# A Mamba-2 scan with an ELU feed-forward behind it: high word of y on ScalarE, scan steps, weight words, loads and output copies moved within their queues

## The chip, the cores and the metric

The kernel runs on one core of a Trainium2 chip. The metric is device time in microseconds, the median of several executions; lower is better. The names are those of the profile: PE is TensorE's matmul row and PEld its weight load, DVE is VectorE, ACT is ScalarE, POOL is GpSimd, SP is the engine whose queue issues nearly all DMAs. Each engine works through its own instructions strictly in program order, so the place of an instruction in its engine's queue matters as much as its length.

## The reference

Two blocks follow each other. The first is a chunked state-space scan over 4 batches, 8 heads, 768 tokens, head size 32, state size 16. The second is a feed-forward layer over all 3072 tokens, with 256 model columns and 2048 hidden ones:

```python
M = CB * L                                   # scores times decays, per chunk and head
y_intra = np.einsum('bhij,bhjd->bhid', M, xc)
y_inter = np.einsum('bhin,bhnd->bhid', Cc, state) * decay_to_i[:, :, :, None]
state = decay_full[:, :, None, None] * state + np.sum(Bx, axis=2)
...
h = x @ w_in                                 # x is y of the scan, one row a token
g = np.where(h > 0.0, h, alpha * (np.exp(np.minimum(h, 0.0)) - 1.0))
return (g @ w_out).astype(np.float32)
```

## The kernel before

**Tiling.** The tokens are cut into 12 blocks of 256. Blocks 0 and 1 fill the pipeline with plain fp32 products; from block 2 on, blocks go in pairs. A *stage* n (4, 6, 8, 10 in the main loop, L1357 on) does three things at once, interleaved by hand: the first feed-forward product and the ELU of pair n, the second product of pair n-2, and the scan of pair m = n+2. After stage 10 a tail does the second product of the last pair.

**Words.** An fp32 product is put together from three passes over rounded words. For y: `y1` is the high word (scaled copy, rounded to fp32r), `y0` the low one (L804), `y_both` a combination (L814); for the weights and for g there are the same three. The passes give `high` and `both`, and the result is `high * (WORD - 1) + WORD * both`.

**Groups.** Inside a stage, k counts 16 *groups*, each 128 hidden columns by 512 tokens, made by `l1_words(n, k, m)` (L819): six matmuls into two PSUM banks, `ps_w` (the `both` sum) and `ps_h` (the `high` one). Then a loop over DVE and ACT closes each group: ACT copies `ps_w` to `e` (L838), DVE finishes the group before it (L861, `end_words`), DVE joins `ps_h` and `e` (the *join*, L844), ACT takes a Relu and an Exp of the joined bank (L854, L855, `begin_end`), and the next group's L861 waits for that Exp. A bank is free again when its last reader is through: `ps_w` after L838, `ps_h` after L861.

**Jobs.** The words of g for the second product are made in three steps spread over two groups: ACT's high word (L916, `first_of_jobs`), DVE's low word (L917, `second_of_jobs`), POOL's combination (L893, `third_of_jobs`). Job q is begun in group q-3 and PE reads it three groups later with twelve short matmuls (L975, two steps of `second`, `l2s(2)`). When a block's sum is complete, `put_out` copies it out: ACT (L981), DVE (L984), then the DMA (L986); its two halves are queued by `put_first` and `put_second`.

**Scan of the next pair.** `stage_scan` places small steps on ACT, DVE, POOL and SP in groups 0 to 10 (POOL's decay masks, L561 and L544, stand in groups 0 to 3). Then come, in this order: `scores` (64 small matmuls, L577, after group 9), `weigh_two` for four quarters (DVE, L586; each frees one bank of scores), `sums` (L607), `states` (DVE L622 and L624, POOL L629), `across` (L654), `inside` in two halves t (L672), and the copies of the result to `yT` (ACT L689 for t = 0, DVE L687 for t = 1). After that, in groups 14 and 15, the words of y are made for the next stage, whose first matmul passes need them.

**PSUM.** Pool `ps_a` has seven banks, `ps_o` has one, used in turn by a sum of `second`, the last quarter of the scores, half of the sums and the last quarter of `across`.

**SP's queue.** `load_words(i)` brings back the words of `w_in` piece i (512 KB, L759, and 256 KB, L760), used by groups 2i and 2i+1. Pieces 0 and 1 of the next stage are loaded in groups 14 and 15, behind a 64-byte DMA named `held` (L1385), which reads a few elements of `yT` and so keeps SP's queue until they are written; piece 2 is loaded in group 0, behind that group's output DMAs. In stage 4 the words of `w_out` pieces 3 to 7 are still being made (`words_of_out`: ACT L902, DVE L903; `low_of_out`: POOL L893).

## Time and profile before

| | |
|---|---|
| median of 3 runs | 347.2 us (346.45 to 347.7) |
| profiled execution, whole | 348.19 us |
| its span (first to last instruction) | 346.5 us |
| granted TensorE clock, mean | 0.999 |
| first stage of the main loop, groups 0 to 15 | 113.9 to 168.0 us |
| stage 6 | 168.0 to 221.5 us |
| stage 8 | 221.5 to 273.9 us |
| stage 10 | 273.9 to 320.2 us |
| tail | 320.2 to 346.5 us |

A stage starts where the trace has the first `ps_h` matmul of its group 0. Busy time by stretch of 20 us (us of work in the stretch):

| stretch | PE | DVE | ACT | POOL |
|---|---|---|---|---|
| 120 to 140 | 20.00 | 15.87 | 17.74 | 16.13 |
| 140 to 160 | 19.03 | 19.14 | 13.97 | 16.60 |
| 160 to 180 | 19.14 | 16.50 | 15.63 | 14.89 |
| 180 to 200 | 19.91 | 19.41 | 16.11 | 16.59 |
| 200 to 220 | 19.63 | 15.20 | 12.95 | 12.75 |
| 220 to 240 | 19.82 | 18.72 | 16.91 | 15.88 |
| 240 to 260 | 20.00 | 17.96 | 15.57 | 13.62 |
| 260 to 280 | 18.80 | 15.96 | 13.91 | 8.78 |
| 280 to 300 | 20.00 | 16.23 | 17.45 | 11.41 |
| 300 to 320 | 20.00 | 18.43 | 16.74 | 13.18 |

How to read the profile's lines: a group's line gives line number, engine, operation, `written<-read` tiles, shapes and count, then busy time and the mean of one in ns, then the idle time before them and what ended it. A line of the timeline begins with start and length in us; a bracket at its end is the idle time of that engine just before, with the work that ended it. Matmuls are pipelined: their rows overlap, and PE counts as busy from the start of one to the modelled end of the next, so a short wait can hide in a busy row.

### The profile page before, as it was taken

To read this page: it belongs to the slowest core of one execution; us is meant where nothing else is said; L and a number is where in the kernel's file an instruction comes from. 1 tells how busy PE (TensorE), PEld (TensorE's weight loads), DVE (VectorE), ACT (ScalarE), POOL (GpSimd) and SP (SyncE) were. 2 spreads that over 40 slices of the span, in tenths; PEclk is the share of its full clock that TensorE was granted. 3 is DMA by queue.
4 is the path that set the end of the run, shared out by engine and by line. 5 is a ranking of instruction groups with operands and counts; after the bars stand their busy time and mean duration, and the time that the engine had idled before them with its cause. 6 is when DMAs were issued, how large, how long until landed. Compare 5 with 4: busy or idle time off the path is not lost.

```text
span 346.5 us, 9640 instructions
## 1 busy us (share of the span) xinstructions
PE 336.4 (97%) x3742; PEld 290.8 (84%) x3742; DVE 288.8 (83%) x511; ACT 258.1 (75%) x533; POOL 214.4 (62%) x242
## 2 busy tenths in 40 slices
PE   8899999999999999899999999999999899999996
PEld 6568888888888888788788888898888799999995
DVE  2898998889997778997999986999986877997951
ACT  4798989599756888866698865797866689897601
POOL 4653554648989396978498858498855245675100
PEclk9999999999999999999999999999999999999999
DMA  8998988472487486631569692569550664160101
GB/s 143 243 218 181 304 174 248 89 134 98 163 159 284 150 241 224 237 101 27 182 180 208 172 305 52 184 196 217 138 182 3 184 208 151 52 199 0 33 0 62
DMA packets 82956, 54.79 MB, mean 158 GB/s; under 512 B 59038, under 2 KB 68574, under 8 KB 82910
## 3 DMA queue, kind: packets, MB, share of 16 engines
q1 hardware_dynamic: 80734, 53.98, 55.8%
q8 instruction: 29, 0.48, 0.6%
q10 hardware_dynamic: 2176, 0.20, 0.5%
q14 instruction: 17, 0.14, 0.1%
HBM read 44.53 MB, written 9.63 MB: 156 GB/s over the span
## 4 chain that ended last, share of the span: by engine, by line
PE 75%; DVE 7%; ACT 5%; SPq 4%; DMA 4%; issue 2%; POOL 1%; DVEq 0%; POOLq 0%; ACTq 0%
PE ps_o L975 18%; PE ps_h L830 14%; PE ps_h L711 11%; PE ps_o L879 11%; PE ps_w L830 8%; PE ps_both L975 6%; DMA w<-w_kept 3%; PE ps_y L672 3%; SPq L184 2%; PE ps_y L654 2%; DVE ps_h L844 2%; PE ps_g L577 2%; DVE g_low L917 1%; ACT e L854 1%; PE ps_st L607 1%
## 5 line engine op out<-in xcount | busy, mean ns | idle before, releaser
L893 POOL TENSOR_TENSOR g_words<-g_words,g_low 128x512 fp32r<-128x512 f32 x62 | 82.5, 1333 | 50.2 <-DVE g_low L917 23.0
L975 PE MATMUL ps_o<-o_words,g_words 128*128 128x256 f32 x448 | 84.0, 285 | 1.0 <-POOL g_words L893 0.9
L975 PEld LDWEIGHTS ps_o<-o_words,g_words 128*128 128x128 f32 x448 | 72.6, 190 | 7.6 <-POOL g_words L893 2.3
L854 ACT ACTIVATE e<-ps_h 128x512 f32<-128x512 f32 x72 | 43.0, 598 | 39.7 <-DVE ps_h L844 39.7
L917 DVE SCALAR_TENSOR_TENSOR g_low<-g_words,g 128x512 fp32r<-128x512 f32 x72 | 64.4, 900 | 0.0
L975 PE MATMUL ps_o<-o_low,g_low 128*128 128x256 f32 x224 | 63.3, 282 | 0.0
L861 DVE SCALAR_TENSOR_TENSOR g<-e,ps_h 128x512 f32<-128x512 f32 x72 | 49.3, 685 | 16.6 <-ACT e L855 15.7
L844 DVE SCALAR_TENSOR_TENSOR ps_h<-ps_h,e 128x512 f32<-128x512 f32 x72 | 49.9, 693 | 5.5 <-ACT e L838 5.0
L838 ACT ACTIVATE e<-ps_w 128x512 f32<-128x512 f32 x72 | 42.0, 583 | 10.6 <-PE ps_w L830 10.5
L830 PE MATMUL ps_w<-y_both,w_words 128*128 128x512 f32 x144 | 48.7, 419 | 0.0
L855 ACT ACTIVATE e<-e 128x512 f32<-128x512 f32 x72 | 45.5, 632 | 2.3
L711 PE MATMUL ps_h<-yT,w_in 128*128 128x256 f32 (+1 forms) x208 | 45.2, 368 | 1.9 <-POOL w_in L254 1.9
L830 PE MATMUL ps_h<-y,w_words 128*128 128x512 f32 x144 | 45.2, 395 | 1.2 <-DVE M L586 0.7
L830 PE MATMUL ps_h<-y,w 128*128 128x512 f32 x144 | 45.2, 394 | 0.8 <-DMA w<-w_kept 0.7
L879 PE MATMUL ps_o<-w_out,g 128*128 128x256 f32 x192 | 45.5, 380 | 0.0
L916 ACT ACTIVATE g_words<-g 128x512 fp32r<-128x512 f32 x72 | 43.6, 623 | 0.0
L711 PEld LDWEIGHTS ps_h<-yT,w_in 128*128 128x128 f32 x208 | 36.3, 190 | 7.7 <-POOL w_in L254 2.9
L975 PEld LDWEIGHTS ps_o<-o_low,g_low 128*128 128x128 f32 x224 | 42.7, 190 | 0.0
L879 PEld LDWEIGHTS ps_o<-w_out,g 128*128 128x128 f32 x192 | 36.1, 189 | 5.4
L830 PEld LDWEIGHTS ps_h<-y,w 128*128 128x128 f32 x144 | 26.8, 188 | 8.2 <-DVE ps_h L844 1.1
L830 PEld LDWEIGHTS ps_h<-y,w_words 128*128 128x128 f32 x144 | 26.8, 188 | 7.8 <-PE ps_w L830 1.1
L830 PEld LDWEIGHTS ps_w<-y_both,w_words 128*128 128x128 f32 x144 | 23.6, 191 | 2.1 <-DVE y_both L814 0.3
(135 smaller groups left out, 554.0 us busy)
## 6 DMA issues: line engine op xcount, KB each, us to landing
w_words<-w_kept SPq DMA_DIRECT2D x28, 512.0 KB
w<-w_kept SPq DMA_DIRECT2D x28, 256.0 KB
L<-flat SPq DMA_DIRECT2D x20, 256.0 KB
w<-in_moe_w_out_dram SPq DMA_DIRECT2D x8, 512.0 KB
w_kept<-w_words SPq DMA_DIRECT2D x8, 512.0 KB
w<-in_moe_w_in_dram SPq DMA_DIRECT2D x7, 512.0 KB
xr<-in_x_dram SPq DMA_DIRECT2D x24, 128.0 KB
out_dram<-eo SPq DMA_DIRECT2D x18, 128.0 KB
```

What stands on the lines that cost most here:

```text
L711: nc.tensor.matmul(out=ps[:, j, toks], lhsT=w_in[i][:, k, j * P:(j + 1) * P], rhs=yT[n // 2][:, k, n % 2].rearrange("p u i -> p (u i)")[:, ...
L830: nc.tensor.matmul(out=ps, lhsT=lhs[:, k], rhs=rhs[:, k], start=k == 0 and lhs is not w0, stop=k == KC - 1 and lhs is not w1)
L838: nc.scalar.activation(e, both, ACT.Copy, scale=WORD)
L844: nc.vector.scalar_tensor_tensor(out=high, in0=high, scalar=WORD - 1.0, in1=e, op0=ALU.mult, op1=ALU.add)
L854: nc.scalar.activation(e, high, ACT.Relu, scale=-1.0)
L855: nc.scalar.activation(e, e, ACT.Exp, scale=-1.0)
L861: nc.vector.scalar_tensor_tensor(out=g_tile(n, m // 2)[:, m % 2].rearrange("p b i -> p (b i)"), in0=e, scalar=1.0, in1=h, op0=ALU.subtract ...
L879: nc.tensor.matmul(out=o_of[n][:, ts], lhsT=g_of[n // 2, j][:, m % 2, n % 2, ts * P:(ts + 1) * P], rhs=w_out[j][:, m % 2], start=(m == 0 a ...
L893: nc.gpsimd.tensor_tensor(out=out, in0=in0, in1=in1, op=ALU.subtract)
L916: yield nc.scalar.activation(words[:, 0], g, ACT.Copy, scale=NEAR / WORD)
L917: yield nc.vector.scalar_tensor_tensor(out=low, in0=words[:, 0].bitcast(F32), scalar=WORD, in1=g, op0=ALU.mult, op1=ALU.subtract)
L975: nc.tensor.matmul(out=ps, lhsT=lhs, rhs=rhs, start=lhs is both_g and first > 0 or lhs is g1 and first > 1, stop=last and lhs is not g1, s ...
```

## The change

- `high_of_y` makes both halves of `y1` on ACT, for every pair; before, DVE made half 0 except for pair 4.
- `l1_words` takes two lists of steps: one run just ahead of the join, one just ahead of `second_of_jobs`.
- In group 10 the third and fourth `weigh_two` run ahead of the join (before: behind the group's `l2s`). `sums` follows group 10 (before: group 11). `states` of the two blocks run in groups 11 and 12 between the join and the job's low word (before: behind those groups' `l2s`).
- `across` follows group 13's matmuls directly, and the step of the second product that stood ahead of it now stands between `across` and the first half of `inside`.
- `first_of_jobs` does the output copies (ACT) ahead of the jobs' high words, `second_of_jobs` does theirs (DVE and the DMA) ahead of the jobs' low words.
- `load_words(2)` is issued ahead of group 0 in stages 6, 8 and 10. `held` reads an element of half t = 0 of `yT` rather than of t = 1.
- In stage 4, `w_out` pieces 3 to 7 are made one a group in groups 2 to 6 (low words in groups 3 to 7), before every second group from 2 to 10 (3 to 11).
- `begin_decays` is dissolved: `decay_sums` (POOL L531) stands at the end of groups 12 and 13 rather than in `stage_scan` of groups 13 and 14. On POOL's queue it keeps its neighbours.

```diff
@@ -788,12 +788,8 @@
     def high_of_y(n):
         y = yT[n // 2].rearrange("p k b u i -> p k (b u i)")
         y1 = big([P, KC, 2 * BLK], F32R, "y1")
-        nc.scalar.activation(y1[:, 1], y[:, 1], ACT.Copy, scale=NEAR / WORD)
-        if n == 4:
-            nc.scalar.activation(y1[:, 0], y[:, 0], ACT.Copy, scale=NEAR / WORD)
-        else:
-            nc.vector.tensor_scalar(
-                out=y1[:, 0], in0=y[:, 0], scalar1=NEAR / WORD, scalar2=None, op0=ALU.mult)
+        for k in range(KC):
+            nc.scalar.activation(y1[:, k], y[:, k], ACT.Copy, scale=NEAR / WORD)
         y_words[n] = y1,
 
     def low_of_y(n):
@@ -816,7 +812,7 @@
                 in1=y[:, k], op0=ALU.mult, op1=ALU.add)
         y_words[n] = y1, y0, both
 
-    def l1_words(n, m, ahead=None):
+    def l1_words(n, m, ahead=None, ahead_of_join=(), ahead_of_jobs=()):
 
 
         cols = slice(m % 2 * P, (m % 2 + 1) * P)
@@ -841,10 +837,14 @@
             end_words()
         if ahead and m == MC - 2 and n > 2:
             high_of_y(ahead)
+        for step in ahead_of_join:
+            step()
         nc.vector.scalar_tensor_tensor(
             out=high, in0=high, scalar=WORD - 1.0, in1=e, op0=ALU.mult, op1=ALU.add)
         if ahead and m == MC - 2 and n > 2:
             low_of_y(ahead)
+        for step in ahead_of_jobs:
+            step()
         if not ahead or m != MC - 2:
             second_of_jobs()
         late.append((n, m, high, e))
@@ -947,20 +947,20 @@
 
     def first_of_jobs():
 
+        while put_first:
+            put_second.append(put_first.pop(0)())
         begun_jobs.append([make() for make in to_begin])
         to_begin.clear()
         for j in begun_jobs[-1]:
             next(j)
-        while put_first:
-            put_second.append(put_first.pop(0)())
 
     def second_of_jobs():
 
+        while put_second:
+            put_second.pop(0)()
         if len(begun_jobs) > 1:
             for j in begun_jobs[0]:
                 next(j)
-        while put_second:
-            put_second.pop(0)()
 
     def third_of_jobs():
 
@@ -1263,13 +1263,6 @@
             words_of_w(5)
             low_of_w(5)
             keep_words(4)
-    def begin_decays(m, k):
-
-        if k < 15:
-            decay_sums(m + k - 13)
-        else:
-            decay_exps(m, 0)
-
     for j in range(8, 16):
         i = j - 8
         l1_words(2, j, 4)
@@ -1319,8 +1312,10 @@
             turn_part(6, 0)
         if i in (3, 4, 7):
             low_of_out((3, 4, 7).index(i))
-        if i > 4:
-            begin_decays(6, i + 8)
+        if i in (5, 6):
+            decay_sums(i + 1)
+        if i == 7:
+            decay_exps(6, 0)
         third_of_jobs()
     end_words()
     low_of_w(1)
@@ -1351,8 +1346,8 @@
             load_b(m + (k > 3))
         if k in (6, 7) and m + 2 < NP:
             load_bc(m + k - 4)
-        if k > 12 and m + 2 < NP:
-            begin_decays(m + 2, k)
+        if k == 15 and m + 2 < NP:
+            decay_exps(m + 2, 0)
 
     for n in range(4, NP, 2):
         m = n + 2 if n + 2 < NP else None
@@ -1374,15 +1369,19 @@
                 to_begin.append(lambda q=k - 13: job(n, q))
             if not m and k in (4, 6, 8, 10, 12, 14, 15):
                 to_begin.append(lambda q=(4, 6, 8, 10, 12, 14, 15).index(k): late_job(q, late_pool))
-            l1_words(n, k, m)
+            if k == 0 and n > 4:
+                load_words(2)
+            l1_words(
+                n, k, m, [lambda q=q: weigh_two(m, q) for q in (2, 3) if m and k == 10],
+                [lambda: states(m + k - 11)] if m and k in (11, 12) else [])
             if n == 4 and k < 2:
                 words_of_w(k + 2)
-            if n == 4 and k in (2, 4, 6, 8, 10):
-                words_of_out(k // 2 + 2)
-            if k in (0, 2, 4, 6, 8, 10) and (k > 2 or n > 4):
+            if n == 4 and 1 < k < 7:
+                words_of_out(k + 1)
+            if k in (2, 4, 6, 8, 10) and (k > 2 or n > 4):
                 load_words(k // 2 + 2)
             if m and k == 14:
-                nc.sync.dma_start(out=held, in_=yT[m // 2][Q:Q + 1, 1, 0, 0, Q:Q + 16])
+                nc.sync.dma_start(out=held, in_=yT[m // 2][Q:Q + 1, 0, 0, 0, Q:Q + 16])
             if m and k > 13:
                 load_words(k - 14)
             if m:
@@ -1391,35 +1390,32 @@
             if n == 4 and k in (1, 2):
                 low_of_w(k + 1)
                 keep_words(k + 1)
-            if n == 4 and k in (3, 5, 7, 9, 11):
-                low_of_out(k // 2 + 2)
-            if k not in (11, 12, 14) or not m:
+            if n == 4 and 2 < k < 8:
+                low_of_out(k)
+            if k != 14 or not m:
                 third_of_jobs()
             if not m:
                 l2s(2)
                 continue
             if k == 9:
                 scores(m, m + 1, pool=p_o, tag="o")
-            l2s((2 - (n == 4 and k < 1), 2, 2, 2, 2, 2, 2, 2, 2, 2, 2, 2, 1, 1, 1, 0)[k])
-            if k in (9, 10):
-                for q in range(2 * k - 18, 2 * k - 16):
+            l2s((2 - (n == 4 and k < 1), 2, 2, 2, 2, 2, 2, 2, 2, 2, 2, 2, 1, 0, 1, 0)[k])
+            if k == 9:
+                for q in range(2):
                     weigh_two(m, q)
-            if k == 10 and m + 2 < NP:
-                for to in (m + 2, m + 3):
-                    spread_cum(to)
-            if k == 11:
+            if k == 10:
+                if m + 2 < NP:
+                    for to in (m + 2, m + 3):
+                        spread_cum(to)
                 sums(m, m + 1, pool=p_o, tag="o")
-                states(m)
-            if k == 12:
-                states(m + 1)
-            if k in (11, 12):
-                third_of_jobs()
             if k == 13:
                 y = across(m, m + 1, pool=p_o, tag="o")
-                l2s(1)
+                l2s(2)
                 inside(y, m, m + 1, t=0)
                 l2s(1)
                 inside(y, m, m + 1, t=1)
+            if k in (12, 13) and m + 2 < NP:
+                decay_sums(m + k - 10)
         if m:
             l2s(3)
         end_words()
```

## The prediction, made before the changed kernel was run

> **What bounds the kernel now.** I read the engines' busy shares first, then PE's waits, then the timeline around each wait, then SP's queue.
>
> ```profile
> PE 336.4 (97%) x3742; PEld 290.8 (84%) x3742; DVE 288.8 (83%) x511; ACT 258.1 (75%) x533; POOL 214.4 (62%) x242
> ```
>
> PE bounds the kernel, so the change can give back only the time in which PE waits. Its waits by releaser (us in total, times, longest) name three causes in the main loop:
>
> ```profile
> PE ps_o L975 <- POOL g_words L893: 0.9, 1, 0.9
> PE ps_h L830 <- DVE M L586: 0.7, 1, 0.7
> PE ps_h L830 <- DMA w<-w_kept: 0.7, 1, 0.7
> PE ps_h L830 <- DMA w_words<-w_kept: 0.5, 1, 0.5
> ```
>
> Rows of pipelined matmuls overlap, so these are too short. I took the distance from one matmul's start to the next and subtracted the steady distance (0.23 us for 512 columns, 0.12 for 256). Above 0.2 us that leaves, from 114 us on: 0.52 (at 142.6) and 0.85 (146.0) in stage 4; 1.03 (169.2), 0.25 (181.1) and 0.57 (214.9) in stage 6; 0.28 (222.9) and 0.22 (237.3) in stage 8; 0.68 and 0.84 (273.1, 274.2) in stage 10. The sum, 5.2 us, is about all that can be won; the tail is PE without a gap.
>
> **Stage 4, group 10.** Timeline:
>
> ```profile
> 142.26 1.12 DVE L903 SCALAR_TENSOR_TENSOR o_words<-o_words,w_out 128x512 fp32r<-128x512 f32 x1
> 142.55 0.58 ACT L838 ACTIVATE e<-ps_w 128x512 f32<-128x512 f32 x1
> 143.18 1.17 PE L577 MATMUL ps_g<-ctm,bct 32*64 32x128 f32 x60 [0.28 <-ACT e L838]
> 144.51 1.81 DVE L917 SCALAR_TENSOR_TENSOR g_low<-g_words,g 128x512 fp32r<-128x512 f32 x1
> 146.24 1.41 DVE L586 TENSOR_TENSOR M<-ps_g,L 128x256 f32<-128x256 f32 x4
> 147.13 0.70 PE L830 MATMUL ps_h<-y,w_words 128*128 128x512 f32 x2 [0.69 <-DVE M L586]
> ```
>
> Scores wait for a bank that ACT's L838 frees, and group 10's `ps_h` for a bank that the first `weigh_two` frees. The change takes L902 and L903 out of groups 8 and 10. Without L903 (1.12) DVE's L861 starts at 142.5, when Exp is done, instead of 143.31; the join follows at 143.1, the low word at 143.7 (1.3 if POOL's o_low no longer runs beside it), weighing at 145.0, and the bank is free at 145.8. PE, with scores at 143.0 (L838 gains only the 0.17 by which L854 stood behind L902), reaches `ps_h` at 146.05: no wait. Gain 147.13 - 146.05 = **1.1**, bounds 0.2 (ACT's part alone) and 1.35 (both gaps). The words move into groups 2 to 6; POOL is idle from 132.81 to 136.25 there (o_low takes 1.3 to 1.75), ACT and DVE have gaps of 0.9 and 0.7 in groups 3 and 5. That cover gone, one 0.63 step on ACT would come back.
>
> **High word of y, start of stages 6, 8 and 10.** Timeline at stage 6:
>
> ```profile
> 164.04 0.62 ACT L791 ACTIVATE y<-yT 128x512 fp32r<-128x512 f32 x1
> 164.21 1.13 DVE L795 TENSOR_SCALAR y<-yT 128x512 fp32r<-128x512 f32 x1
> 165.86 1.28 DVE L804 SCALAR_TENSOR_TENSOR y<-y,yT 128x512 fp32r<-128x512 f32 x2
> 165.98 0.60 ACT L854 ACTIVATE e<-ps_h 128x512 f32<-128x512 f32 x1 [1.31 <-DVE ps_h L844]
> 169.09 1.28 POOL L893 TENSOR_TENSOR g_words<-g_words,g_low 128x512 fp32r<-128x512 f32 x1 [4.04 <-DVE g_low L917]
> 170.42 0.51 PE L975 MATMUL ps_o<-o_words,g_words 128*128 128x256 f32 x2 [0.86 <-POOL g_words L893]
> ```
>
> DVE runs without a gap from the `yT` copies through L861, L795, the join, L804, L814 to the low word of job 0; POOL and PE wait for it. Without L795 the row moves up by 1.13. The second half on ACT costs 0.62 and falls into ACT's gap of 1.31; it ends at about 165.3, when the second L804 needs it. I take 0.95 for stage 6; in stage 8 (L795 0.46) 0.38. PE arrives at 169.40, POOL at 170.37 - 0.95: the 1.03 goes nearly whole. But POOL is full afterwards: 13.13 of the 14 us from 171 to 185, and 13.11 from 224 to 238, with job 5's words just in time (184.81 for 185.00; 237.74 for 237.80). Here the output copies cost something: put ahead of the low word of job 2 they delay it by two L984 (0.75), and POOL, which was free 0.5 after that row's end (174.06 for 173.54), waits some 0.25. So job 5's words come 0.7 and 0.14 sooner, which with the slack above would let PE gain 0.9 and 0.2; stage 8's next wait, scores on L838, gains with the loop. **0.95** in stage 6 (0.4 to 1.28, both its gaps) with piece 2's load, late at 181.1, included; **0.4** in stage 8 (0 to 0.5).
>
> The Trainium skill (ScalarE: Activation LUTs, Rules for kernel authors) speaks against this move: a plain multiplication belongs on VectorE, not ScalarE. By that rule, with this trace's 0.62 on ACT against 0.42 for the shortest L795, each such start would lose 0.2, and the sum below would be 1.6 instead of 3.3. The trace agrees with it on the lengths; here DVE is the engine without a gap and ACT has one.
>
> **Loads.** Timeline of SP, then of PE, at the start of stage 10:
>
> ```profile
> 268.85 0.24 SPq L1385 DMA_DIRECT2D held<-yT  x1
> 269.62 1.83 SPq L760 DMA_DIRECT2D w<-w_kept  x1
> ```
>
> ```profile
> 273.87 0.70 PE L830 MATMUL ps_h<-y,w_words 128*128 128x512 f32 x2 [0.52 <-DMA w_words<-w_kept]
> 275.26 0.71 PE L830 MATMUL ps_h<-y,w 128*128 128x512 f32 x2 [0.68 <-DMA w<-w_kept]
> ```
>
> `held` goes when DVE has written half 1 of `yT` (268.82); half 0 is done by ACT at 266.95. The DMAs were all but idle from 260 to 270 (at most 8 GB/s), so the pieces land 1.87 sooner, at 272.0 and 273.4, for PE at 273.2 and 273.7. Gain of both gaps, less a little at the next job: **1.4**; 0 if `load_words(0)` then waits for its buffers, 1.5 at most. Piece 2, issued in stage 6 at 174.81 right behind the output DMAs, is no longer behind DVE; its buffers come free with group 15's matmuls. Three loads in a row on SP's queue then hold up only output DMAs and loads needed later.
>
> **Scan, groups 10 to 13.** Weighing (4 x 0.33 from start to start) now lies between L861 and the join of group 10, the states (4 x 0.33) behind the joins of 11 and 12. DVE's sum is the same, and the window in which ACT does Relu and Exp (1.25) is filled by other work. `across` moves ahead by one step of `second` (0.71). Its four banks: two sums, `ps_h` of groups 12 and 13 and three of its own make seven, so it must wait for L838 of group 13. Two rows before and one of it:
>
> ```profile
> 261.99 0.63 ACT L855 ACTIVATE e<-e 128x512 f32<-128x512 f32 x1
> 262.53 0.58 ACT L838 ACTIVATE e<-ps_w 128x512 f32<-128x512 f32 x1
> 263.24 0.91 PE L654 MATMUL ps_y<-bct,Sx 32*64 32x64 f32 x64
> ```
>
> L838 ended at 263.11 and `across` began at 263.24: the step ahead of it covered the wait. Now PE arrives at 262.44 and waits 0.6, with two steps of `second` and `inside` queued behind, so that `inside` comes 0.5 later in stage 8. In stages 4 and 6 `across` itself took 1.16 and 1.46, waiting for states; these now come sooner, and the balance is 0.15 against and 0.15 for. Together **-0.5**; bounds -1.8 (three waits of 0.6) and +0.8 (no wait, and the 0.25 and 0.55 over 0.91 gone). `sums` finds its banks at 148.3, 201.6 and 254.5, PE there at 148.5, 202.4 and 255.3: nothing. `decay_sums` keeps its place in POOL's queue and its price (2.4 and 1.9): nothing, unless POOL waited for its input.
>
> **Sum.** 1.1 + 0.95 + 0.4 + 1.4 - 0.5 = 3.3 us off the profiled execution of 348.19 (span 346.5, 1.7 around it), so 344.9. That execution lies 1.0 above the median, and from the median, 347.2, it gives 343.9. The 0.57 at 214.9 ("issue") I leave alone.
>
> **Rivals.**
> *A, POOL and the PSUM banks take half back:* no gain at stages 6 and 8 beyond the 0.4 and 0 of their lower bounds, `across` at -1.2: 1.1 + 0.4 + 1.4 - 1.2 = 1.7, so 345.5. For it: POOL's 13.1 of 14 us. Against: nothing is added on POOL.
> *B, the loads come no sooner,* held by buffers: 1.4 falls away, 345.3. For it: other L759 rows have waited for PE. Against: behind `held` the next load always followed within 0.35 us, so its buffers were free by then.
> *C, the closing loop becomes the bound in the scan (slower):* the four weighs ahead of the join of group 10 delay Relu, Exp and L838 by 1.33, and `across` adds 0.6; three stages, 5.8 us. If PE then had no free bank, that would eat the 3.8 of the other parts and leave +2.0: 349.2. It decides from the point where the loop trails PE by more than a group, 2.8 us. For it: the loop trails by 3 to 4.5 in stage 4's first groups. Against: in group 10 L838 starts only 0.66 after its `ps_w` (146.48 for 145.82), as PE is held by scores.
> *D, ScalarE is the wrong place:* the second half on ACT makes L804 wait and stages 6 and 8 lose 0.2 each: 1.1 - 0.4 + 1.4 - 0.5 = 1.6, 345.6. For it: 0.62 against 0.42. Against: the gap of 1.31. The rule of the Trainium skill named above (ScalarE: Activation LUTs, Rules for kernel authors) is this case.
> *E, nothing moves:* each wait is handed to the next engine: 347.2.
>
> **How the numbers follow.** Forecast 0.50; A 0.12, B 0.08, C 0.17, D 0.05, E 0.08. A difference of 0.3% (1.04 us) is about what a measurement of this kernel can tell from none, so faster means below 346.16. The forecast and A, B, D lie below it but for tails of 0.03: faster 0.72. Within: E, the tails, a mild C: 0.12. Slower: most of C with some of E: 0.16. The range: the upper bounds with half of the scan's 0.8 give 1.35 + 1.28 + 0.5 + 1.5 + 0.4 = 5.0, so low 342.2; high 347.3 takes in A, B, D and E and leaves out most of C (0.15), with 0.04 below. The forecast's own range is 342.2 to 345.4.
>
> **What would show it.** Right: no PE wait over 0.3 us at the first L975 of stages 6 and 8, none on `w_kept` at stage 10, `ps_h` of stage 4's group 10 without a wait on L586, and a wait of about 0.5 ahead of L654. Wrong: L838 of group 10 more than 2 us behind its `ps_w`, or `held` moved and the load behind it not.

## The result, and the profile after

The changed kernel takes 345.16 us (median of 6 runs, 344.49 to 345.4) beside 347.57 for the kernel before (6 runs): ratio 0.993, 95% interval 0.9911 to 0.9949. That is 2.4 us less; 3.3 were forecast. The profiled execution took 345.40 us, with a span of 343.6 (before: 348.19 and 346.5).

The diff moves some lines of the code. In the changed kernel L834 is the L838 of before, L842 the join L844, L826 the L830, L800 and L810 the L804 and L814, L792 the high word of `y` (L791 and L795 before) and L1384 `held` (L1385). All other lines named here kept their numbers.

The busy times of the changed kernel, as shares of the span:

```profile
PE 334.7 (97%) x3742; PEld 289.5 (84%) x3742; DVE 285.1 (83%) x507; ACT 259.7 (76%) x537; POOL 215.9 (63%) x242
```

DVE lost 3.7 us and ACT gained 1.6; POOL gained 1.5 though nothing was added to it. PE's waits (by what it waited for: total, times, longest):

```profile
PE ps_y L654 <- ACT e L834: 1.3, 3, 0.5
...
PE ps_g L577 <- ACT e L834: 0.7, 1, 0.7
```

The waits on POOL's words, on L586 and on the loads are gone from this list. `across` (L654) stands in it for the first time, three times, one for each scan; and the scores (L577) wait longer than before.

**Where the time went.** To compare two traces I took the start of the first `ps_w` matmul of each group and subtracted that of the other trace. The start of the kernel, which the change doesn't touch, differs between any two executions: at the last L711 the changed kernel was already 0.47 us ahead of the one before. So experiments are read from group 1 of stage 4 on, unless it is said otherwise. From there on the changed kernel is 1.94 us sooner.

| stretch | forecast | changed kernel less the one before, us |
|---|---|---|
| up to the last L711 | 0 | -0.47, code not changed |
| from there to group 1 of stage 4 | 0 | -0.42 |
| stage 4, groups 1 to 14 | -0.95 | -0.03 |
| start of stage 6 | -0.95 | -0.99, then +0.31 at jobs 4 and 5 |
| scan of stage 6 | -0.15 | -0.26 |
| start of stage 8 | -0.4 | -0.38, then +0.35 at jobs 4 and 5 |
| scan of stage 8 | +0.5 | +0.59 |
| start of stage 10 | -1.4 | -1.53 |
| to the end | 0 | 0 |
| sum | -3.3 | -2.83 |

(The forecast gave 0.5 later for `inside` in stage 8 and 0.15 against and for in stages 4 and 6; here they stand with their stages.)

### The profile page after: what moved, and what is told of

It is laid out like the page before. It is cut to its first block, busy times and chain, and to the rows that moved or that the text cites. A ratio compares the mean times of both kernels' runs of the same rounds, so it can differ in the third digit from the quotient of the medians.

```text
span 343.6 us, 9637 instructions
## 1 busy us (share of the span) xinstructions
PE 334.7 (97%) x3742; PEld 289.5 (84%) x3742; DVE 285.1 (83%) x507; ACT 259.7 (76%) x537; POOL 215.9 (63%) x242
## 4 chain that ended last, share of the span: by engine, by line
PE 47%; ACT 20%; DVE 17%; issue 6%; SPq 4%; POOL 3%; DMA 2%; DVEq 0%; POOLq 0%; ACTq 0%
PE ps_o L975 13%; PE ps_h L711 9%; PE ps_h L826 7%; PE ps_both L975 6%; DVE ps_h L842 5%; ACT e L854 5%; ACT e L855 5%; PE ps_w L826 4%; ACT e L834 3%; DVE g L861 2%; DVE g_low L917 2%; PE ps_o L879 2%; PE ps_y L672 2%; DVE y L800 2%; ACT L L538 2%
## 5 line engine op out<-in xcount | busy, mean ns | idle before, releaser
L893 POOL TENSOR_TENSOR g_words<-g_words,g_low 128x512 fp32r<-128x512 f32 x62 | 81.9, 1324 | 51.0 <-DVE g_low L917 28.5
L975 PE MATMUL ps_o<-o_words,g_words 128*128 128x256 f32 x448 | 84.3, 286 | 0.3
L975 PEld LDWEIGHTS ps_o<-o_words,g_words 128*128 128x128 f32 x448 | 72.1, 190 | 7.6 <-POOL g_words L893 3.2
L861 DVE SCALAR_TENSOR_TENSOR g<-e,ps_h 128x512 f32<-128x512 f32 x72 | 49.3, 685 | 17.9 <-ACT e L855 14.6
L917 DVE SCALAR_TENSOR_TENSOR g_low<-g_words,g 128x512 fp32r<-128x512 f32 x72 | 63.5, 888 | 0.0
L975 PE MATMUL ps_o<-o_low,g_low 128*128 128x256 f32 x224 | 63.3, 283 | 0.0
L842 DVE SCALAR_TENSOR_TENSOR ps_h<-ps_h,e 128x512 f32<-128x512 f32 x72 | 49.8, 692 | 4.5 <-ACT e L834 2.8
L834 ACT ACTIVATE e<-ps_w 128x512 f32<-128x512 f32 x72 | 42.0, 583 | 9.8 <-PE ps_w L826 9.7
L826 PE MATMUL ps_w<-y_both,w_words 128*128 128x512 f32 x144 | 48.6, 419 | 0.0
L711 PE MATMUL ps_h<-yT,w_in 128*128 128x256 f32 (+1 forms) x208 | 45.1, 367 | 2.0 <-POOL w_in L254 2.0
L826 PE MATMUL ps_h<-y,w_words 128*128 128x512 f32 x144 | 45.2, 394 | 0.0
L826 PE MATMUL ps_h<-y,w 128*128 128x512 f32 x144 | 44.7, 391 | 0.0
L711 PEld LDWEIGHTS ps_h<-yT,w_in 128*128 128x128 f32 x208 | 36.3, 190 | 7.7 <-POOL w_in L254 2.7
L975 PEld LDWEIGHTS ps_o<-o_low,g_low 128*128 128x128 f32 x224 | 42.7, 190 | 0.0
L826 PEld LDWEIGHTS ps_h<-y,w 128*128 128x128 f32 x144 | 27.0, 188 | 6.3
L826 PEld LDWEIGHTS ps_h<-y,w_words 128*128 128x128 f32 x144 | 26.9, 188 | 6.0
L826 PEld LDWEIGHTS ps_w<-y_both,w_words 128*128 128x128 f32 x144 | 23.6, 191 | 1.9 <-DVE y_both L810 0.2
```

The source lines that it names most:

```text
L711: nc.tensor.matmul(out=ps[:, j, toks], lhsT=w_in[i][:, k, j * P:(j + 1) * P], rhs=yT[n // 2][:, k, n % 2].rearrange("p u i -> p (u i)")[:, ...
L826: nc.tensor.matmul(out=ps, lhsT=lhs[:, k], rhs=rhs[:, k], start=k == 0 and lhs is not w0, stop=k == KC - 1 and lhs is not w1)
L834: nc.scalar.activation(e, both, ACT.Copy, scale=WORD)
L842: nc.vector.scalar_tensor_tensor(out=high, in0=high, scalar=WORD - 1.0, in1=e, op0=ALU.mult, op1=ALU.add)
L861: nc.vector.scalar_tensor_tensor(out=g_tile(n, m // 2)[:, m % 2].rearrange("p b i -> p (b i)"), in0=e, scalar=1.0, in1=h, op0=ALU.subtract ...
L893: nc.gpsimd.tensor_tensor(out=out, in0=in0, in1=in1, op=ALU.subtract)
```

## The profile after, place by place

**Stage 4, groups 9 and 10**, timeline of the changed kernel:

```profile
142.19 0.58 ACT L834 ACTIVATE e<-ps_w 128x512 f32<-128x512 f32 x1
...
142.82 1.18 PE L577 MATMUL ps_g<-ctm,bct 32*64 32x128 f32 x60 [0.72 <-ACT e L834]
...
144.43 1.41 DVE L586 TENSOR_TENSOR M<-ps_g,L 128x256 f32<-128x256 f32 x4
...
145.46 0.63 PE L826 MATMUL ps_w<-y_both,w_words 128*128 128x512 f32 x2
...
145.93 0.62 PE L826 MATMUL ps_h<-y,w_words 128*128 128x512 f32 x2
...
146.12 0.60 ACT L834 ACTIVATE e<-ps_w 128x512 f32<-128x512 f32 x1 [1.20 <-PE ps_w L826]
```

The second gap went as forecast: `ps_h` of group 10 follows `ps_w` by the steady 0.47, with no wait on L586. The first one grew: the distance between two score matmuls exceeds the steady one by 0.97 us where it was 0.52. L834 of group 10 starts 0.66 behind its `ps_w`, so PE is ahead of the closing loop by no more than before (rival C).

**Start of stage 6**, timeline of the changed kernel, DVE and ACT:

```profile
162.73 0.69 DVE L861 SCALAR_TENSOR_TENSOR g<-e,ps_h 128x512 f32<-128x512 f32 x1
...
163.12 1.14 ACT L792 ACTIVATE y<-yT 128x512 fp32r<-128x512 f32 x2
...
163.33 0.69 DVE L842 SCALAR_TENSOR_TENSOR ps_h<-ps_h,e 128x512 f32<-128x512 f32 x1
...
163.94 1.28 DVE L800 SCALAR_TENSOR_TENSOR y<-y,yT 128x512 fp32r<-128x512 f32 x2
```

The join follows L861 directly; the multiplication of 1.13 us that stood between them is on ACT, in the gap that ACT had there, and DVE's L800 doesn't wait for it.

**Scan of stage 8**, timeline of the changed kernel:

```profile
260.56 0.58 ACT L834 ACTIVATE e<-ps_w 128x512 f32<-128x512 f32 x1
260.58 0.34 PE L654 MATMUL ps_y<-bct,Sx 32*64 32x64 f32 x8
...
261.29 0.84 PE L654 MATMUL ps_y<-bct,Sx 32*64 32x64 f32 x56 [0.36 <-ACT e L834]
```

Eight matmuls of `across` go, then PE stands until ACT has emptied `ps_w` of group 13 (261.14). From start to start the gaps are 0.62, 0.68 and 0.56 us above the steady distance in the three scans.

**Start of stage 10**, SP's timeline of the changed kernel:

```profile
265.68 0.24 SPq L1384 DMA_DIRECT2D held<-yT  x1
266.01 0.33 SPq L759 DMA_DIRECT2D w_words<-w_kept  x1
266.45 0.37 SPq L760 DMA_DIRECT2D w<-w_kept  x1
```

`held` goes 3.17 us sooner than before; 1.30 of that is the kernel's lead at that point, and 1.87, as forecast, is the change. No matmul waits for a load there any more. The second issue takes 0.37 where it took 1.83; this turns out to matter.

## Experiments

Twelve kernels, each one edit to the changed kernel unless said otherwise. "Sooner" and "later" are against the changed kernel, from group 1 of stage 4 to the end.

**1. `across` behind one step of `second` again** (four executions):

```diff
-            l2s((2 - (n == 4 and k < 1), 2, 2, 2, 2, 2, 2, 2, 2, 2, 2, 2, 1, 0, 1, 0)[k])
+            l2s((2 - (n == 4 and k < 1), 2, 2, 2, 2, 2, 2, 2, 2, 2, 2, 2, 1, 1, 1, 0)[k])
...
                 y = across(m, m + 1, pool=p_o, tag="o")
-                l2s(2)
+                l2s(1)
```

> The changed kernel with one step of the second product put back ahead of across (and one, not two, behind it). Theory (each part's worth is the PE wait it removes or makes): the three waits of across on ACT's copy of ps_w, 0.62 + 0.68 + 0.56 us in the changed kernel's trace, are covered by the step of 0.71, so PE reaches the tail 1.5 to 1.9 us sooner, counted from group 1 of stage 4. Rival (the closing loop of DVE and ACT sets the pace there, and hands every gain to the next wait): less than 0.5 us.

Measured: 343.77 us, ratio to before 0.9876 (0.9814 to 0.9938). The gain lies at the three places and nowhere else: 0.59, 0.45 and 0.64 sooner between groups 13 and 14, and 1.72 in all. Its timeline in the scan of stage 8:

```profile
259.90 0.58 ACT L834 ACTIVATE e<-ps_w 128x512 f32<-128x512 f32 x1
...
260.63 0.91 PE L654 MATMUL ps_y<-bct,Sx 32*64 32x64 f32 x64
```

L834 has ended (260.48) when `across` begins, and all 64 matmuls go in one run, as in the kernel before. So the step ahead of `across` was the cover for its bank.

**2. The copies of the output behind the low words and the closing steps again** (the order of `put_first` and `put_second` as before):

```diff
     def first_of_jobs():
-        while put_first:
-            put_second.append(put_first.pop(0)())
         begun_jobs.append([make() for make in to_begin])
...
     def second_of_jobs():
-        while put_second:
-            put_second.pop(0)()
         if len(begun_jobs) > 1:
```

> The changed kernel with the output copies behind the jobs' words again, on ACT and DVE. Theory (POOL's chain of jobs 1 to 5 is delayed by the copies): job 2's combination starts 0.25 us sooner, the waits of PE at jobs 4 and 5 (0.35 and 0.37 less some 0.2 of steady distance, in stages 6 and 8) shrink by 0.25 a stage, together 0.5 us sooner. Rival (the copies free PSUM banks that PE or the scores need): 0 to 0.5 us later.

Measured, one execution: 343.97 us; 0.34 sooner at jobs 4 and 5 in each of stages 6 and 8, where 0.25 was expected. POOL's timeline at the start of stage 6, first of the changed kernel:

```profile
170.44 1.39 POOL L544 TENSOR_SCALAR_AFFINE_SELECT L<-L 64x512 f32<-64x512 f32 x2
172.51 1.31 POOL L893 TENSOR_TENSOR g_words<-g_words,g_low 128x512 fp32r<-128x512 f32 x1 [0.69 <-DVE g_low L917]
```

and of this kernel:

```profile
169.74 1.73 POOL L544 TENSOR_SCALAR_AFFINE_SELECT L<-L 64x512 f32<-64x512 f32 x2
171.55 1.30 POOL L893 TENSOR_TENSOR g_words<-g_words,g_low 128x512 fp32r<-128x512 f32 x1
```

In the changed kernel POOL waits 0.69 us for the low word that DVE writes behind two L984 (0.75); in this one it doesn't wait, though its L544 pair is 0.34 longer. POOL has no slack up to job 5, so the difference, 0.35, reaches PE. Besides, 0.47 were won between groups 9 and 10 of stage 4, where no copies are; more on this below.

**3. `held` on half 1 of `yT` again:**

```diff
-  nc.sync.dma_start(out=held, in_=yT[m // 2][Q:Q + 1, 0, 0, 0, Q:Q + 16])
+  nc.sync.dma_start(out=held, in_=yT[m // 2][Q:Q + 1, 1, 0, 0, Q:Q + 16])
```

> The changed kernel with held reading half 1 of yT again. Theory: the waits for w_kept at the start of stage 10 come back, 1.4 to 1.5 us, and nothing changes at stages 6 and 8. Rival (piece 0 comes in time anyway, since the other edits free SP's queue sooner): 0 to 0.3 us.

Measured, one execution: 346.15 us, and only 0.36 later at the start of stage 10. SP's timeline of this kernel:

```profile
267.97 0.24 SPq L1384 DMA_DIRECT2D held<-yT  x1
268.31 0.34 SPq L759 DMA_DIRECT2D w_words<-w_kept  x1
268.75 0.37 SPq L760 DMA_DIRECT2D w<-w_kept  x1
269.22 1.42 SPq L759 DMA_DIRECT2D w_words<-w_kept  x1
```

`held` did go late. But the issue of the low half of piece 0 (L760) took 0.37 and not 1.83; here the long issue is the next one, for piece 1, which nobody waits for yet. What SP did meanwhile shows in the DMA queues of this kernel between 269 and 271 us (packets, MB, share):

```profile
q1 hardware_dynamic: 109, 0.42, 81.1%
q8 instruction: 1, 0.02, 2.9%
```

One transfer of 16 KB of instructions starts at 269.33, inside the long issue. In the kernel before one starts at 269.69 and takes 1.39, inside L760's 1.83. So of the two waits there, 1.5 us in all, 0.36 comes from a late `held` by itself, and the rest goes with a long issue in piece 0, beside which an instruction fetch began. The kernel of experiment 6, whose `held` is on half 1 too, repeats this. Its SP timeline, then a row of PE:

```profile
266.22 0.24 SPq L1381 DMA_DIRECT2D held<-yT  x1
266.56 0.33 SPq L759 DMA_DIRECT2D w_words<-w_kept  x1
267.00 1.57 SPq L760 DMA_DIRECT2D w<-w_kept  x1
```

```profile
272.51 0.70 PE L826 MATMUL ps_h<-y,w 128*128 128x512 f32 x2 [1.29 <-DVE g_low L913]
```

(`held` is L1381 in that file.) From start to start this wait is 1.46. The matmul reads `y` and `w`, not the `g_low` that the bracket names; the last part of L760's load landed at 272.37, 0.14 ahead of it, as in the kernel before (275.12 and 275.26). A 16 KB instruction transfer begins 0.02 us after that issue.

**4. `held` on half 0, alone, in the kernel before:** the same edit, the other way round.

> The kernel before with held reading half 0 of yT and nothing else. Theory (the pieces land as much sooner as held lets them go, 1.87 us): the two waits at stage 10 go, 1.4 to 1.5 us sooner. Rival (held is worth only the 0.4 us that undoing it cost, and the rest of the wait came from the long issue of the second DMA, 1.83 us, which lies beside an instruction fetch): 0.3 to 0.5 us sooner if the fetch stays at that DMA.

Measured, one execution: 347.26 us; the start of stage 10 came 1.20 sooner than before, nearer to the theory. Its five issues there take 0.24 to 0.38, so none is long. Ahead of group 12 of stage 10 PE then lost 0.45, at 307.72: the words of `w_in` for that group, issued at 301.81, landed at 307.58. In the kernel before the same load lands 0.26 ahead of its matmul; why it comes later beside PE here stays open. Over all traces: in the eleven with `held` on half 0, the four loads behind it are issued in 0.33 to 0.38 each, no fetch begins among them, and no matmul waits for them. In the three with half 1 (before, experiments 3 and 6) a fetch begins among them and one of them is long. So the edit is worth 0.36 where the long issue misses piece 0, and up to 1.5 where it falls on it. No kernel had an early `held` and a long issue in piece 0, so whether the lead of 1.87 would cover one isn't shown.

**5. Half 0 of y's high word on DVE again** (for all pairs but 4):

```diff
-        for k in range(KC):
-            nc.scalar.activation(y1[:, k], y[:, k], ACT.Copy, scale=NEAR / WORD)
+        nc.scalar.activation(y1[:, 1], y[:, 1], ACT.Copy, scale=NEAR / WORD)
+        if n == 4:
+            nc.scalar.activation(y1[:, 0], y[:, 0], ACT.Copy, scale=NEAR / WORD)
+        else:
+            nc.vector.tensor_scalar(
+                out=y1[:, 0], in0=y[:, 0], scalar1=NEAR / WORD, scalar2=None, op0=ALU.mult)
```

> The changed kernel with half 0 of y's high word on DVE again for pairs 2, 6, 8 and 10. Theory (DVE's row without a gap is lengthened by that instruction): the first step of the second product waits again at stage 6 (0.7 to 1.0 us) and at stage 8 (0.2 to 0.4), nothing at stage 10; in stage 2 0.3. Together 1.0 to 1.6 us later. Rival (ScalarE is the wrong place for a multiplication): 0.2 us sooner a start.

Measured, one execution: 347.19 us; 0.32 later at the start of each of stages 6, 8 and 10, 0.97 in all, where 0.7 to 1.0 had been expected at stage 6 and nothing at stage 10. Ahead of that it lost 0.28 between groups 8 and 9 of the loop before stage 4, and 0.12 at group 1 of stage 4. Its timeline at stage 6:

```profile
163.83 0.42 DVE L795 TENSOR_SCALAR y<-yT 128x512 fp32r<-128x512 f32 x1
...
164.17 0.69 DVE L846 SCALAR_TENSOR_TENSOR ps_h<-ps_h,e 128x512 f32<-128x512 f32 x1
```

(L846 is the join in this file.) DVE's row takes 0.42 here, not the 1.13 of the kernel before. POOL's L531 (1.94 in both) explains it: here it had ended at 163.77, ahead of the row; in the kernel before it ran to 165.05, and the row, begun at 164.21, ended 0.29 behind it. So undoing the edit inside the changed kernel couldn't tell what it had brought.

**6. The high word wholly on ScalarE, alone, in the kernel before** (the first hunk of the change and nothing else):

> The kernel before with one edit: the high word of y entirely on ScalarE (both halves), all else as before. In the changed kernel, putting the second half back on DVE cost 0.33 at each of the three stage starts, where DVE's row took 0.42. In the kernel before that row took 1.13 at the start of stage 6, beside GpSimd. Theory (the edit by itself takes DVE's whole row away, 1.13, as the prediction reckoned): the start of stage 6 comes 0.9 to 1.0 sooner and gives 0.25 to 0.35 of it back at jobs 4 and 5. Rival (most of the 1.0 measured at that start came from work that the scan's new order takes off DVE ahead of it): the start comes only 0.2 to 0.4 sooner. At stage 8 both expect 0.3 to 0.4, given back; at stage 10 nothing or little, as PE waits there for the loads.

Measured, one execution: 345.69 us, with the kernel before at 346.98 on that chip. The start of stage 6 came 0.95 sooner, the size of the forecast's term, and none of it was given back at jobs 4 and 5, where the copies are as before. The start of stage 8 came 0.33 sooner. Ahead of group 1 of stage 4 it won 0.28 and 0.14 at the two places of experiment 5. From group 1 on it is 1.64 sooner than before; the whole change, from the same point, is 1.94 sooner. In that 1.64, 0.22 at the scores of stage 4 and 0.20 in the scan of stage 6 lie where the edit changes no instruction. So this one small edit brings most of what the whole change brings; the rest nearly cancels.

**7. The words of w_out in groups 2, 4, 6, 8, 10 again:**

```diff
-            if n == 4 and 1 < k < 7:
-                words_of_out(k + 1)
+            if n == 4 and k in (2, 4, 6, 8, 10):
+                words_of_out(k // 2 + 2)
...
-            if n == 4 and 2 < k < 8:
-                low_of_out(k)
+            if n == 4 and k in (3, 5, 7, 9, 11):
+                low_of_out(k // 2 + 2)
```

> The changed kernel with w_out's words in every second group again. Theory: the 0.63 us by which the loop falls behind in groups 4 and 5 of stage 4 goes, but ACT's and DVE's steps in groups 8 and 10 come back, with the wait of ps_h on the first weighing (0.85): by group 12 PE is 0.4 us later. Rival (the words only change places, and what they cost in groups 4 and 5 is what they saved): within 0.1 us.

Measured, one execution: 347.82 us (1.47 of its lateness had come before group 1 of stage 4). In stage 4 it is 0.46 sooner at the scores, 0.91 later at `ps_h` of group 10, which waits for L586 again as in the kernel before (0.36 later by group 12, as the theory had it), and 0.52 later behind `across`: 0.96 later in all. The 0.52 is POOL's. Its timeline:

```profile
155.27 1.29 POOL L893 TENSOR_TENSOR o_low<-w_out,o_words 128x512 fp32r<-128x512 f32 x1
156.53 1.28 POOL L893 TENSOR_TENSOR g_words<-g_words,g_low 128x512 fp32r<-128x512 f32 x1
157.78 1.49 POOL L629 TENSOR_TENSOR Sx<-S_new,hmask 128x64 f32<-128x64 f32 x4
```

The low word of group 11 stands ahead of the second block's L629 on POOL, whose `Sx` is what `across` reads. They start 0.26 after `across` has begun (157.51); in the changed kernel they start 0.87 before it.

**8. The scan's steps where they were** (weighing, sums, states and `across`; the rest as changed):

```diff
-            l1_words(
-                n, k, m, [lambda q=q: weigh_two(m, q) for q in (2, 3) if m and k == 10],
-                [lambda: states(m + k - 11)] if m and k in (11, 12) else [])
+            l1_words(n, k, m)
...
+            if k in (9, 10):
+                for q in range(2 * k - 18, 2 * k - 16):
+                    weigh_two(m, q)
...
+            if k == 11:
+                sums(m, m + 1, pool=p_o, tag="o")
+                states(m)
+            if k == 12:
+                states(m + 1)
```

> The changed kernel with weighing, sums, states and across where they were before. Theory (only across exposes a wait, the other moves are hidden): stage 8 0.6 us sooner, stage 6 0.3 later, stage 4 0.1 either way: 0.2 to 0.5 us sooner in all. Rival (the weighing ahead of the join of group 10 holds up the closing loop, 1.33 us a stage): 2 to 4 us sooner.

Measured, one execution: 344.95 us, 0.92 sooner: 0.31, 0.33 and 0.59 in the scans (groups 9 to 14), less 0.23 and 0.13 at the starts of stages 6 and 8. Experiment 1 won 1.72 by `across` alone, so by subtraction the other steps of the new order are worth some 0.8 the other way. Rival C's 2 to 4 us aren't there.

Between groups 9 and 14 of stage 4, experiments 7 and 8 make a square, against the kernel before: both parts changed -0.12; words alone (8) -0.12 - 0.31 = -0.43; scan alone (7) -0.12 + 0.96 = +0.84. All four kernels enter stage 4 alike (the loop trails by 4.52 to 4.54 at group 1). The parts don't add up: together they are 0.53 better than their sum (+0.41), and that is the 0.52 of POOL's queue in experiment 7, which the scan's new order loses while the low word of group 11 is in its way.

**9. The load of piece 2 behind the words of group 0 again:**

```diff
-            if k == 0 and n > 4:
-                load_words(2)
...
-            if k in (2, 4, 6, 8, 10) and (k > 2 or n > 4):
+            if k in (0, 2, 4, 6, 8, 10) and (k > 2 or n > 4):
```

> The changed kernel with the load of piece 2 back behind the words of group 0 in stages 6 and 8 (instead of ahead of them). Theory (the prediction: in the kernel before PE waited 0.25 for this piece at group 4 of stage 6 since SP's issue stood behind the output copies that DVE delayed; it is worth at most that): stage 6 loses 0 to 0.25 at group 4, stage 8 nothing. Rival (the earlier load matters to SP's queue, in which later issues and the output copies follow it): a loss above 0.3 in a stage or a gain of over 0.1.

Measured, one execution: 346.07 us, of which 0.45 came before group 1 of stage 4; no stage differs by more than 0.1 after it. In the changed kernel the earlier load is worth nothing.

**10. `across` and the copies as before** (the edits of 1 and 2 together, four executions):

> Both edits at once on the changed kernel: one step of the second product ahead of across again, and the output copies behind the jobs' words again. Alone they gave 1.7 us (the waits of across) and 0.6 us (POOL's chain in stages 6 and 8), with 0.5 more in stage 4 that had no output copy to explain it. Theory (the waits are separate): 2.2 to 2.4 us sooner than the changed kernel from group 1 of stage 4 on. Rival (across sooner done lets PE run into POOL's chain, which takes part back): 1.7 us or less.

Measured: 343.25 us, ratio 0.9878 (0.9846 to 0.991); 2.90 sooner from group 1 of stage 4, made of 0.49 at the scores, 0.33, 0.72 and 0.64 in the scans and 0.35 and 0.37 at jobs 4 and 5. The two faults add up: alone the edits gave 1.72 and 1.19. The scores still wait 0.49. By their ratios to before (0.9876 and 0.9878) experiments 1 and 10 can't be told apart; the copies' part is read from the traces.

**Why the scores wait.** In the changed kernel the closing loop trails PE by 2.94 us at group 6 of stage 4, in the kernel before by 2.29. The step is in group 4. POOL's timeline of the changed kernel:

```profile
127.89 2.53 POOL L893 TENSOR_TENSOR o_low<-w_out,o_words 128x512 fp32r<-128x512 f32 x2
130.38 1.49 POOL L476 TENSOR_TENSOR ctm<-bct,hmask 128x512 f32<-128x512 f32 x1
```

and DVE's beside it:

```profile
129.22 1.75 DVE L903 SCALAR_TENSOR_TENSOR o_words<-o_words,w_out 128x512 fp32r<-128x512 f32 x1
130.89 0.67 DVE L468 STREAM_TRANSPOSE bct<-bc 128x256 f32<-128x256 f32 x1
131.39 0.69 DVE L861 SCALAR_TENSOR_TENSOR g<-e,ps_h 128x512 f32<-128x512 f32 x1
```

L903 takes 0.68 when POOL is idle. Here it starts just behind the second of two L893 (one takes 1.28), and ends 0.55 us after that pair has ended (130.42). L861 reads `ps_h` from PSUM and is not held up: it takes its 0.69 inside POOL's L476.

In the kernels of experiments 2 and 10 the loop enters stage 4 closer to PE (4.33 at group 1, for 4.53), POOL's two L893 start sooner beside PE (in experiment 2 by 0.76 and 0.44), L903 of groups 3 and 4 take 1.18 and 1.34, and the loop trails by 2.46 and 2.45 at group 6: that is the 0.47 of experiment 2. Up to there each engine has the same instructions in the same order in the kernel of experiment 2 and in the changed one, so it is a matter of how the rows happen to meet. Why the loop enters closer stays open. Two more kernels put the words elsewhere.

**11. Words in groups 2, 3, 5, 6, 7** (on the kernel of 10):

```diff
-            if n == 4 and 1 < k < 7:
-                words_of_out(k + 1)
+            if n == 4 and k in (2, 3, 5, 6, 7):
+                words_of_out(k + 1 - (k > 4))
...
-            if n == 4 and 2 < k < 8:
-                low_of_out(k)
+            if n == 4 and k in (3, 4, 6, 7, 8):
+                low_of_out(k - (k > 4))
```

> The best version so far (across behind one step of second, copies as before) with the words of w_out in groups 2, 3, 5, 6, 7 instead of 2 to 6 (the low words one group later each, so 3, 4, 6, 7, 8). Theory (DVE's L903 of group 4 collides with GpSimd's low word and mask, 1.34 to 1.75 instead of 0.68, and the closing loop carries that lag to the scores of group 9, which wait 0.49 in the best version so far and 0.97 in the changed kernel): the loop's lag at group 6 falls below 2.4 and the wait of the scores below 0.3, 0.3 to 0.5 us less through group 10. Rival (the lag is set by the number of L903 in a row, not by where they lie beside GpSimd; words in groups 6 and 7 are nearer to the scores): the wait stays at 0.5 or grows, 0 to 0.6 later.

Measured, one execution: 343.06 us; 0.46 later than the kernel of 10. The loop trails by 1.93 at group 6, as the theory had it (0.25 of that was there at group 1, 4.07 for 4.32), but the scores wait 1.09. Its timeline:

```profile
137.75 1.74 POOL L893 TENSOR_TENSOR o_low<-w_out,o_words 128x512 fp32r<-128x512 f32 x1
...
138.26 1.78 DVE L903 SCALAR_TENSOR_TENSOR o_words<-o_words,w_out 128x512 fp32r<-128x512 f32 x1
...
139.97 0.68 DVE L861 SCALAR_TENSOR_TENSOR g<-e,ps_h 128x512 f32<-128x512 f32 x1
...
143.08 1.17 PE L577 MATMUL ps_g<-ctm,bct 32*64 32x128 f32 x60 [0.84 <-ACT e L834]
```

The same collision, in group 7: L903 begins inside L893 (until 139.49) and ends 0.55 after it (140.04). The time came out as the rival said (0 to 0.6 later). Its reason, the number of L903 in a row, is not what the rows show: the L903 of groups 2, 3, 5 and 6 take 0.68, 1.17 (beside a mask of POOL), 0.69 and 0.68, and the fifth, which meets L893, takes 1.78. So the mechanism is the theory's, and the edit put it three groups nearer to the scores.

**12. GpSimd's low words in groups 3, 5, 7, 8, 9** (on the kernel of 10, four executions):

```diff
-            if n == 4 and 2 < k < 8:
-                low_of_out(k)
+            if n == 4 and k in (3, 5, 7, 8, 9):
+                low_of_out((3, 5, 7, 8, 9).index(k) + 3)
```

> The best version so far (across behind one step of second, copies as before, words of w_out in groups 2 to 6) with GpSimd's low words of w_out in groups 3, 5, 7, 8, 9 instead of 3 to 7, so that none is issued in groups 4 and 6, where DVE writes a word of its own. Theory (DVE's L903 is long, 1.34 to 1.78, where it starts inside a GpSimd L893 of 512 columns, and that delay reaches the scores): L903 of groups 4 and 6 takes below 1.1, the loop's lag at group 6 is below 2.2, and the scores of group 9 wait below 0.3 instead of 0.49; 0.2 to 0.5 us less. Rival (a GpSimd L893 lengthens whatever DVE runs beside it, so the low words of groups 8 and 9, nearer to the scores, stretch DVE's rows there instead): the wait of the scores, or that of ps_h of group 10 behind them, grows by 0.2 to 0.8, no time won.

Measured: 342.47 us (342.32 to 342.85), ratio to before 0.9865 (0.9849 to 0.9882), the shortest of all. The five L903 take 0.68, 1.18, 1.06, 0.69 and 0.69; the loop trails by 2.31; the scores wait 0.40. The theory had said below 2.2 and 0.3; the sign is the theory's, the size below it: 0.19 sooner than the kernel of 10 from group 1 of stage 4 on, while the medians, from two chips, differ by 0.8. As the meeting of rows alone moved 0.47 in experiment 2, a gain over the kernel of 10 isn't shown. From group 1 of stage 4 on this kernel is 5.03 us sooner than the one before, where the forecast had found 5.2 us of waits. In group 4, first POOL's timeline, then DVE's:

```profile
128.80 1.04 POOL L476 TENSOR_TENSOR ctm<-bct,hmask 128x512 f32<-128x512 f32 x1
129.79 1.73 POOL L893 TENSOR_TENSOR o_low<-w_out,o_words 128x512 fp32r<-128x512 f32 x1
```

```profile
129.32 1.06 DVE L903 SCALAR_TENSOR_TENSOR o_words<-o_words,w_out 128x512 fp32r<-128x512 f32 x1
```

L903 starts inside POOL's mask and ends 0.54 after it; the L893 behind the mask is long in its turn (1.73) and ends 1.14 after L903. After the other has let go, each needs its own undisturbed length less some 0.13 to 0.16.

## Why the prediction was right, and where not

Direction and range held. Of the five terms of the sum, the starts of stages 6 and 8 and the scan came with their mechanism, the loads with half of it, and stage 4's did not come. The time is 1.3 us above the forecast of 343.9. Some 0.4 of that is the kernel before, whose median beside it was 347.57 for 347.2. By the number alone rivals B (345.3), A (345.5) and D (345.6) lie nearer to 345.16 than the forecast; only the traces decide between them.

Some luck is in it too. From group 1 of stage 4 on 1.94 of the 3.3 came: 0.92 is missing in stage 4 and 0.66 at jobs 4 and 5. That the trace is 2.83 shorter as a whole is due to 0.89 from ahead of that point, on which the forecast had not counted and of which 0.47 lies where no code was changed.

**Start of stages 6 and 8.** Right in mechanism and size: 0.99 and 0.38 came, against 0.95 and 0.4, and experiment 6 shows that the edit alone brings the 0.95. Also right that POOL is then full and the output copies cost something; POOL waited 0.69 where the forecast had some 0.25, and PE paid 0.34 in each stage (experiment 2). The forecast had counted this into its 0.95 and 0.4, so what was off is a size: net 0.68 and 0.03, both inside the bounds given. Of piece 2's load the forecast made a part of the 0.95; experiment 9 shows nothing of it.

Rival A (POOL takes half back) came true in part: its 0.4 and 0 at the two starts stand against net 0.68 and 0.03, so in stage 8 nearly all was taken back. But it needs the output copies ahead of the low words: with the copies as before, experiment 6 gave nothing back.

Rival D fell. The Trainium skill (ScalarE: Activation LUTs, Rules for kernel authors) would leave multiplications to VectorE. The lengths agree with it (1.14 for two on ACT, 0.42 for one on DVE in experiment 5), the time doesn't: experiment 6 gained 0.95 and 0.33 us at the starts of stages 6 and 8 by going against it, since DVE had no gap there and its row at stage 6 took 1.13 beside POOL.

**Missed.** The same edit acts ahead of the main loop, on the words of pair 2: 0.26 to 0.28 us between groups 8 and 9 in three traces (the change, experiments 5 and 6), and in no trace whose edit leaves it alone. The same three have another 0.12 to 0.14 at group 1 of stage 4; there kernels with the same code differ by up to 0.2 as well, so that part isn't shown. The forecast looked at the starts of stages 6, 8 and 10 alone.

**Stage 4, the step that failed.** The 1.1 was the gap behind L586 (0.85) and some 0.2 of the one at the scores, which would close as L902 and L903 left groups 8 and 10. The first closed. The second grew from 0.52 to 0.97. The step that failed is the cover of the words' new places. The forecast took POOL for idle there; POOL's timeline of the kernel before shows for how much of "there" that is so:

```profile
128.23 1.30 POOL L893 TENSOR_TENSOR o_low<-w_out,o_words 128x512 fp32r<-128x512 f32 x1
129.47 1.05 POOL L476 TENSOR_TENSOR ctm<-bct,hmask 128x512 f32<-128x512 f32 x1
130.47 1.74 POOL L893 TENSOR_TENSOR o_low<-w_out,o_words 128x512 fp32r<-128x512 f32 x1
132.18 0.62 POOL L423 TENSOR_TENSOR b_tok<-b_tok,eb 128x256 f32<-128x256 f32 x1
136.24 1.60 POOL L893 TENSOR_TENSOR g_words<-g_words,g_low 128x512 fp32r<-128x512 f32 x1 [3.44 <-ACT e L854]
```

It is idle from 132.81 to 136.25, as the forecast read, but full, without a gap of 0.1, from 119.8 until then, and three of the five L903 moved into that stretch (123.93, 126.60 and 129.22 in the changed kernel, which is 0.9 ahead there). In group 4 POOL had two L893 in a row where L903 came: DVE lost 1.07 there, the loop trailed by 0.65 more at group 6, and 0.45 of it was left at the scores. The forecast had named the price of a failed cover, one step of 0.63.

Words alone gave 0.43 (experiment 8), so most of the miss is theirs. The forecast also added the terms for words and scan as if they were independent. They aren't, but that isn't where the time went: together they are better than their sum.

**Scan.** `across` does wait for L834 of group 13, since seven banks are held: right. The forecast's -0.5 weighed 0.5 in stage 8 against a balance in stages 4 and 6; measured were 0.59, 0.45 and 0.64 for `across` (experiment 1), a loss in each scan, offset by 0.8 that the other steps of the new order won (experiment 8). Net about -0.9: the right sign, inside its bounds of -1.8 and +0.8, and 0.4 more than the forecast. Rival C fell with experiment 8; the loop kept 0.66 behind `ps_w`.

**Loads.** 1.53 came, for 1.4; `held` went the forecast 1.87 sooner relative to the loop. But the reason was half told: the forecast put the lateness on `held`, and the row beside it, an issue of 1.83 us, was read as part of the same delay. Experiment 3 shows that without that long issue in piece 0 the old `held` costs 0.36. That 1.53 and not 0.36 came was luck as far as the forecast goes: it had not priced where the long issue falls. Rival B fell: the loads followed `held` by 0.33. Rival E fell with the interval of the ratio.

**What would show it.** All four signs came: no wait above 0.3 at the first L975 of stages 6 and 8, none on the loads, none on L586, and 0.56 to 0.68 within L654. Two of the parts, `across` and the copies, each cost time by themselves, and without them, with the low words spread (experiment 12), the rest of the change is worth 1.35% instead of 0.7%.

## What to carry to other kernels

Cost an engine's row by what else runs at that moment, and after a move look at the rows where it lands: the gain was in taking a row of 1.13 off the engine without a gap, the loss in putting 0.68 us where it became 1.75. When a step is moved ahead by one step of filler, count the buffers held at that moment; the filler may have been the cover of the last one. And undoing one part of a change tells its worth only within the rest: try the part alone as well (0.32 by undoing, 0.95 alone, at the same place).

## What the runs showed of the hardware

**Some rows of DVE and POOL shut each other out.** L903 takes 0.68 alone, and 1.06, 1.75 and 1.78 where POOL's row had begun first; in those three it ends 0.54 to 0.55 after POOL's row, whatever the overlap. The 1.13 of L795 in the kernel before ends 0.29 behind POOL's L531, and alone it takes 0.42. Where DVE came first, POOL's 1.3 became 1.73. Rows that read one operand from PSUM are not held up: of the 66 L861 in the changed kernel from stage 4 on, 46 start inside a row of POOL, and none takes more than 0.70. The Trainium skill (SBUF — State Buffer, SBUF: two separate sides) describes the port pair that the two share as a lock held for a whole instruction by whichever starts first. The held-up rows agree with that, and give a way to work out such a length: the other's remaining time, plus one's own less some 0.13.

**Long DMA issues lie beside instruction fetches.** The issues of the loads at the start of stage 10 take 0.33 to 0.38 us, and 1.83, 1.42 and 1.57 (the kernel before, experiments 3 and 6) in the three beside which a 16 KB instruction transfer started (0.07, 0.12 and 0.02 us after them). Where it falls differs from kernel to kernel. In the changed kernel the three loads from `w_kept` that took over 1 us between stages 4 and 10 all lie within 0.3 us of such a transfer; in the kernel before, three of five do, so it isn't the only reason for a long issue. No run took the fetch away by itself; this is read from their coinciding.

**The start differs.** Up to the last L711 the code is the same in all these kernels, and the traces lie there between 0.85 ahead of the kernel before and 1.0 behind it. A single execution is therefore read by its stretches, not by its total. In the main loop, stretches that an edit leaves alone mostly agree within 0.1 us, but some have moved by up to 0.47 (the scores of stage 4 in experiment 2, several places in experiment 4), so a smaller difference at one place of one trace is no proof of an effect.
